# First block of x on ScalarE's transfer queue, and TensorE's warm-up on a tile of zeros with one product less

## The chip, the cores and the metric

The kernel runs on one core of one Trainium2 chip. Five engines work side by side and each runs its own list of instructions in order: TensorE (PE, with its weight loads as PEld), VectorE (DVE), ScalarE (ACT), GpSimd (POOL) and SyncE (SP). Transfers are issued by an engine's queue and are carried by the core's 16 DMA engines. The metric is the device time of one execution in microseconds (us), lower is better.

## The reference

One block of tokens x (2048 tokens of 448 values) goes through two attentions of 16 heads with 28 values each, and the two results are mixed by a gate per token.

```
g = sigmoid(sum(x * gate_w))
A:  q, k, v = split(x @ A_wqkv)                       # 16 heads of 28
    phi(t) = [softmax(t @ w_phi), softmax(-(t @ w_phi))]
    a = (phi(q) (phi(k)^T v)) / (phi(q) sum(phi(k)) + 1e-6) @ A_wo
B:  q, k, v = split(x @ B_wqkv)
    b = softmax(q k^T / sqrt(28)) v @ B_wo
out = g * a + (1 - g) * b
```

All inputs are float32. A is a linear attention, B an ordinary one with 2048 x 2048 scores per head.

## The kernel before

Values are split into a high part in a short format (`fp32r`) and a low rest, and a product is made of three passes: high times high, high times the weight's low part, and x's low part times high. x lies transposed in SBUF as `XH` (high) and `XL` (low), in four blocks `b` of 128 of the 448 input values (the last block holds 64 of them twice, high and low) and four tiles `t` of 512 tokens.

The stages are: the projection of q and k of attention B (28 units, a unit being 128 outputs by 512 tokens; results go out to DRAM as `qkd`); beside it and behind it the folding of `w_phi` into the A weights (`pwk`), the values and features of attention A, and the row maxima for B's softmax (`mx_unit`, from products `pmd` and `pmb`); then the long loop of B over scores (`g`), exponentials (`p`) and values (`pv`); last the output projection.

The order on TensorE, VectorE, ScalarE and GpSimd is that of the program text (`tc.manual_schedule` names these four). SyncE is not among them: the order of its queue, which issues the loads and stores, is set by the framework's planner from its own estimate of when each one is wanted and when its buffer is free. Each transfer counts on one of eight semaphores in turn, so a transfer also waits until the one eight places before it has landed.

`first_units` (L580 to L616) is the start. It issues eight loads of 256 KB, by turns a block of the weights `wqkB` (L585) and a block of x's first tile (L586), into `first_raw0` to `first_raw3`, and then the two loads of x's second tile (L132, by `x_loads`), which reuse the buffers of the first blocks. While these travel, TensorE runs eight 128 x 128 products of the identity matrix `ident` with itself into a PSUM bank that is overwritten later (L591); `ident` is made by GpSimd. Then, for each block b, ScalarE casts the weights to their high part (L594), VectorE (block 0) or ScalarE (the others) casts x (L595), VectorE forms the two low parts (L596, L598, and L601 for the last block), and TensorE runs 12 products of 128 x 512 (8 for the last block) into four PSUM banks (L608). After the four blocks the results are copied and written out by `keep_qk` (L546, L547, L548), through four buffers `ev` that are free again when their write has landed.

The other units follow in `proj_qk` (L109). Around them the transfers of SyncE's queue bring x's third and fourth tile (L132, L323), `phi_s` (L626), the weights `wkA` to be folded (`wtk`, L355), the second weights `wB1` in two halves (L132, cast at L143), `wvA`, and two small constants `sel_s` and `mask_s` (L633, L634). GpSimd's one small copy at L353 writes into `wtk` from `phi_s`, so the loads of `wtk` wait for it and it waits for `phi_s`. Later `qp`, `kp` and `kt` are loaded from `qkd` (L176), GpSimd subtracts (L206), and the first `pmd` product (L260) uses them.

`red` is a 128 x 128 tile that VectorE sets to zero at the start (L163) and that the row maxima use later.

Of the kernel before, what the change touches and what calls it, by code (L numbers as in the profile page):

```python
# [17 lines left out]
P = 128  # L18
# [18 lines left out]
def f32(ap):  # L37
    return ap.bitcast(F32)
# [3 lines left out]
def gated_mix_kernel(ctx, tc, xT, wqkB, wvB, wvA, wkAT, wqAT, phi, woA, woB,  # L42
# [7 lines left out]
    nc = tc.nc  # L50
# [12 lines left out]
    def ps_s(nm):  # L63
        return ps.tile([P, 512], F32, tag="s", name=nm, bufs=psn[0])

    def ps_pv(nm):
        return ps.tile([P, 512], F32, tag="pv", name=nm, bufs=1)

    def ps_mx(nm):
        return ps.tile([P, 512], F32, tag="mx", name=nm, bufs=psn[1])  # L70
# [12 lines left out]
    ident = const.tile([P, P], F32, name="ident")  # L83
# [78 lines left out]
    red = mxp.tile([P, 128], F32R, name="red", bufs=1)  # L162
# [380 lines left out]
    def keep_qk(m, t, pq, ev):  # L543
        tt = slice(t * 512, (t + 1) * 512)
        e = ev.tile([P, 2, 512], F32R, tag="ev", name=f"ev{t}_{m}")
        nc.scalar.copy(e[:, 0, :], pq)  # L546
        nc.vector.tensor_sub(e[:, 1, :], pq, f32(e[:, 0, :]))  # L547
        nc.sync.dma_start(qk_d[m * P:(m + 1) * P, :, tt], f32(e))  # L548
# [14 lines left out]
    def x_loads(t):  # L563
        loads(("x", t), lambda: load_x(t, 0), lambda: load_x(t, 2))
# [7 lines left out]
    def splits(n):  # L572

        if n % 4 == 1 and n < 12:
            split_x(n // 4 + 1, raws.pop(("x", n // 4 + 1)))
        if n in (13, 15):
            split_part(wB[1], "wB1", 384, (n - 13) // 2)
        take_lows()

    def first_units():  # L580

        raw = [stg.tile([P, 2, 512], F32, tag="stg", name=f"first_raw{b}") for b in range(3)]
        raw.append(f32(ev.tile([P, 2, 512], F32R, tag="ev", name="first_raw3")))
        for b in range(4):
            nc.sync.dma_start(raw[b][:, 0, :], wqkB[:, b, :512])  # L585
            nc.sync.dma_start(raw[b][:, 1, :], xT[:, b, :512])  # L586
        x_loads(1)
        pqs = [ps_s(f"pqk0_{m}") for m in range(3)] + [ps_pv("pqk0_3")]
        later.extend(ps_mx(f"pqk_{i}") for i in range(3))
        for _ in range(8):  # L590
            nc.tensor.matmul(pqs[3][:, :P], ident, ident, start=True, stop=True)  # L591
        for b in range(4):
            w, x = wB[0][:, :, b, :], XH[:, b, :512]
            nc.scalar.copy(w[:, 0, :], raw[b][:, 0, :])  # L594
            (nc.scalar.copy if b else nc.vector.tensor_copy)(x, raw[b][:, 1, :])  # L595
            nc.vector.tensor_sub(w[:, 1, :], raw[b][:, 0, :], f32(w[:, 0, :]))  # L596
            if b < 3:
                nc.vector.tensor_sub(XL[:, b, :512], raw[b][:, 1, :], f32(x))  # L598
                todo = [(0, x), (1, x), (0, XL[:, b, :512])]
            else:  # L600
                nc.vector.tensor_sub(x[64:], raw[b][64:, 1, :], f32(x[64:]))  # L601
                todo = [(0, x), (1, x)]
            if b < 3:
                order = [(i, m) for i in range(3) for m in range(4)]
            else:
                order = [(i, m) for m in range(4) for i in range(2)]
            for i, m in order:
                nc.tensor.matmul(pqs[m], w[:, todo[i][0], m * P:(m + 1) * P], todo[i][1],  # L608
                                 start=b == 0 and i == 0, stop=b == 3 and i == 1,
                                 skip_group_check=True)  # L610
        hold = raws[("x", 1)][0][:1, 0, :4]
        splits(1)
        nc.gpsimd.tensor_copy(phi_s[:1, :, 0], hold)
        for m in range(4):
            keep_qk(m, 0, pqs[m], ev)

    later = []
    first_units()
    pkv = ps_pv("pkv")
    for n in range(4, NP):  # L620
# [588 lines left out]
```

## Time and profile before

| what | us |
|---|---|
| median of 3 runs (984.8 to 987.25) | 984.94 |
| the profiled execution's own time | 984.67 |
| its span, first to last instruction | 982.9 |
| TensorE busy | 976.8 (99%) |
| ScalarE busy | 752.8 (77%) |
| VectorE busy | 727.6 (74%) |
| GpSimd busy | 235.4 (24%) |

In the rows shown below, a merged row gives the start, the length, the engine, the line, the operation, what is written from what, the shapes, how many instructions were merged, and in brackets the idle time before it with what ended that. SPq is SyncE's queue issuing a transfer; the length is that of the issue, not of the transfer. A row with "x4: 187/188/333" gives the number of instructions and their shortest, median and longest duration in ns, then the first and last start. A row that begins with two times and a colon is a stretch: its length, the busy time of PE, PEld, DVE, ACT and POOL with the number of instructions, TensorE's granted clock, the share of the DMA engines' time in use, and GB/s. The end of a TensorE row is modelled, so the distance from one start to the next tells more than its length.

### The profile page before, as it was taken

The page shows a single profiled execution, that of the slowest core. Times are in us where ns is not written, and L with a number is a line of the kernel's source. Part 1 is how long each engine was busy: PE and PEld are TensorE (multiplying, and loading weights), DVE is VectorE, ACT ScalarE, POOL GpSimd, SP SyncE. Part 2 cuts the span into 40 slices and gives each one's busy share as a digit, 9 for nine tenths or more (in the row PEclk, how much of TensorE's full clock was granted, in tenths as well). Part 3 has the DMA queues.
Part 4 walks back from the last instruction along what each step waited for, and adds up shares of the span by engine and source line. Part 5 has one row for each costly group of instructions (what it writes and reads, how often), then busy time and mean ns, then how long its engine had stood idle before and what let it go on. Part 6 is the DMA issues. An engine that isn't in the chain of part 4 may idle for free.

```text
span 982.9 us, 22267 instructions
## 1 busy us (share of the span) xinstructions
PE 976.8 (99%) x8384; PEld 606.0 (62%) x8384; DVE 727.6 (74%) x1335; ACT 752.8 (77%) x1442; POOL 235.4 (24%) x224
## 2 busy tenths in 40 slices
PE   9999999999999999999999999999999999999998
PEld 8877877787777665555555555555555555555555
DVE  5566767799765678888888888888888888885112
ACT  5455655578776688898898898898898898897662
POOL 1235435578734710031011011011011011010010
PEclk9999999999999999999999999999999999999999
DMA  9973110013233233121132121122231222100441
GB/s 306 324 233 117 37 53 32 23 47 99 73 103 111 89 121 126 40 59 40 65 91 69 42 61 41 60 77 71 70 82 41 64 63 63 40 24 31 141 150 57
DMA packets 56139, 84.47 MB, mean 86 GB/s; under 512 B 17216, under 2 KB 23984, under 8 KB 56032
## 3 DMA queue, kind: packets, MB, share of 16 engines
q1 hardware_dynamic: 56032, 83.06, 27.1%
q8 instruction: 66, 1.08, 0.5%
q14 instruction: 41, 0.34, 0.1%
HBM read 54.86 MB, written 27.78 MB: 84 GB/s over the span
## 4 chain that ended last, share of the span: by engine, by line
PE 96%; DVE 3%; issue 0%; ACT 0%; POOL 0%; DVEq 0%; POOLq 0%; ACTq 0%
PE g L830 29%; PE pv L975 27%; PE pqk L109 6%; PE poa L109 4%; PE pk L127 4%; PE pva L127 4%; PE g L288 3%; PE pmd L260 3%; PE pob L109 3%; PE pvb L127 2%; PE pvb L109 2%; PE pq L109 2%; PE pn L507 1%; PE pqk L608 1%; PE pft L495 1%; PE poL L1008 1%
## 5 line engine op out<-in xcount | busy, mean ns | idle before, releaser
L838 ACT ACTIVATE p<-g 128x512 f32<-128x512 f32 x1020 | 525.7, 608 | 82.5 <-PE g L830 81.8
L295 DVE TENSOR_REDUCE part<-g 128x1 f32<-128x512 f32 x704 | 442.2, 683 | 84.4 <-PE g L288 83.8
L830 PEld LDWEIGHTS g<-qst,kst 32*128 32x128 f32 x3060 | 220.9, 182 | 215.3 <-DVE part L295 194.4
L830 PE MATMUL g<-qst,kst 32*128 32x512 f32 x3060 | 337.6, 419 | 0.1
L975 PE MATMUL pv<-p,vb 128*32 128x512 f32 x2048 | 273.0, 604 | 0.0
L288 PE MATMUL g<-kc,qc 28*128 28x512 f32 x704 | 233.2, 494 | 0.0
L394 POOL TENSOR_TENSOR oUb<-oUb,rsb 128x512 f32<-128x512 f32 x15 | 19.3, 1286 | 490.9 <-DMA rsb<-rdb 423.8
L265 DVE CUSTOM_DVE_ANT_0 rl<-pmb,rl 128x512 f32<-128x512 f32 x160 | 103.2, 682 | 43.7 <-ACT rl L264 43.7
L264 ACT ACTIVATE rl<-pmd 128x512 f32<-128x512 f32 x160 | 87.4, 601 | 31.3 <-PE pmb L260 29.0
L288 PEld LDWEIGHTS g<-kc,qc 28*128 28x128 f32 x704 | 86.2, 181 | 0.2
L975 PEld LDWEIGHTS pv<-p,vb 128*32 128x32 f32 x2048 | 40.5, 108 | 66.1 <-issue 64.8
L109 PE MATMUL pqk<-XH,wB 128*128 128x512 f32 x192 | 59.1, 396 | 0.0
L546 ACT CAST ev<-pqk 128x512 fp32r<-128x512 f32 x28 | 16.1, 589 | 39.8 <-PE pqk L109 28.7
L986 DVE SCALAR_TENSOR_TENSOR acc<-pob,gate,acc 128x448 f32<-128x448 f32 x12 | 8.2, 684 | 48.3 <-PE pob L109 48.3
L109 PE MATMUL poa<-woA_s,oTa 128*128 128x448 f32 x192 | 43.5, 375 | 0.0
L260 PE MATMUL pmb<-kp,qp 28*128 28x512 f32 x160 | 42.0, 495 | 0.7 <-DVE part L265 0.3
L547 DVE TENSOR_TENSOR ev<-pqk,ev 128x512 fp32r<-128x512 f32 x28 | 19.0, 689 | 31.0 <-ACT ev L546 31.0
L109 PEld LDWEIGHTS pqk<-XH,wB 128*128 128x128 f32 x192 | 35.4, 188 | 8.6 <-issue 1.5
L260 PE MATMUL pmd<-kp,qp 28*128 28x512 f32 x160 | 39.9, 494 | 0.0
L127 PE MATMUL pk<-wkA_s,XH 128*128 128x448 f32 x128 | 39.4, 381 | 0.0
L109 PEld LDWEIGHTS poa<-woA_s,oTa 128*128 128x128 f32 x192 | 34.9, 188 | 6.3 <-issue 2.9
L127 PE MATMUL pva<-wvA_s,XH 128*128 128x450 f32 x128 | 37.8, 371 | 0.0
(154 smaller groups left out, 1085.8 us busy)
## 6 DMA issues: line engine op xcount, KB each, us to landing
qkd<-ev SPq DMA_DIRECT2D x28, 512.0 KB
qst<-qkd SPq DMA_DIRECT2D x64, 112.0 KB
kst<-qkd SPq DMA_DIRECT2D x64, 112.0 KB
od<-oTb SPq DMA_DIRECT2D x48, 112.0 KB
rsa<-rda SPq DMA_DIRECT2D x8, 512.0 KB
oL<-od SPq DMA_DIRECT2D x8, 512.0 KB
rsb<-rdb SPq DMA_DIRECT2D x15, 256.0 KB
gad<-ga SPq DMA_DIRECT2D x16, 224.0 KB
```

What stands on the lines that cost most here:

```text
L109: nc.tensor.matmul(dst, l, r, start=i == 0, stop=i == len(todo) - 1)
L127: nc.tensor.matmul(dst[:, :n], l, r, start=i == 0, stop=i == len(todo) - 1, skip_group_check=True)
L260: nc.tensor.matmul(pm[j], qc[js, qt * P:(qt + 1) * P], kc[js, :], start=True, stop=True, tile_position=(32 * i, 0))
L264: nc.scalar.activation(rl, pm[i], AF.Relu)
L265: nc.vector.tensor_tensor_reduce(rl, pm[2 + i], rl, 1.0, LOWEST, ALU.add, ALU.max, part[:, col + i:col + i + 1])
L288: nc.tensor.matmul(pm, mxs[("qc", gq)][js, qt * P:(qt + 1) * P], mxs[("kc", gq // NQ, kb)][js, :], start=True, stop=True, tile_position=(3 ...
L295: nc.vector.tensor_reduce(part[:, col:col + 1], pm, AX.X, ALU.max)
L394: (nc.gpsimd if n == 1 else nc.vector).tensor_mul(oU, oU, rs)
L547: nc.vector.tensor_sub(e[:, 1, :], pq, f32(e[:, 0, :]))
L830: nc.tensor.matmul(st[j], kst_of[(gq // NQ, kt // 4)][js, k, (kt % 4) * P:(kt % 4 + 1) * P], qst_of[gq][js, q, :], start=n == 0, stop=n == ...
L838: nc.scalar.activation(p, st[j], AF.Exp, scale=SCALE)
L975: nc.tensor.matmul(pv[32 * j:32 * j + 32, :], vb[kt // 8][:, kt % 8, 4 * g + j, :], pt[j], start=kt == 0, stop=kt == NT - 1, tile_position ...
```

## The change

```
         for b in range(4):
             nc.sync.dma_start(raw[b][:, 0, :], wqkB[:, b, :512])
-            nc.sync.dma_start(raw[b][:, 1, :], xT[:, b, :512])
+            (nc.sync if b else nc.scalar).dma_start(raw[b][:, 1, :], xT[:, b, :512])
         x_loads(1)
         pqs = [ps_s(f"pqk0_{m}") for m in range(3)] + [ps_pv("pqk0_3")]
         later.extend(ps_mx(f"pqk_{i}") for i in range(3))
-        for _ in range(8):
-            nc.tensor.matmul(pqs[3][:, :P], ident, ident, start=True, stop=True)
+        for _ in range(7):
+            nc.tensor.matmul(pqs[3][:, :P], f32(red), f32(red), start=True, stop=True)
```

The load of x's first block is issued by ScalarE as its first instruction, ahead of the table load that its first cast brings. The warm-up products read `red` in place of `ident`, and there are seven. Apart from these, the order on TensorE, VectorE, ScalarE and GpSimd is the same.

On SyncE's queue the planner puts out another order for the first fifty or so transfers. Before (left) and after (right), a name once for each transfer or group:

```
before                                  after
wqkB 0, x 0, wqkB 1, x 1, ... x 3       wqkB 0, wqkB 1, x 1, ... x 3
                                        x tile 3 block 0
x tile 1 (2 loads)                      x tile 1 (2 loads)
x tile 2 first load                     x tile 2 first load
x tile 3 blocks 0, 1                    x tile 3 blocks 1, 2
x tile 2 second load                    x tile 2 second load
x tile 3 blocks 2, 3                    x tile 3 block 3
phi_s, wB1 first half, sel_s, mask_s
qkd x7                                  qkd x8
                                        phi_s, wB1 first half
wtk x1, qkd x1, wtk x3, qkd x2          qkd x1, wtk x4, qkd x1
wB1 second half, qkd, qp, kp, kt        wB1 second half, qkd, qp, kp, kt
qkd x3, wvA x2                          qkd x3, wvA x2, sel_s, mask_s
```

## The prediction

> **What bounds the kernel.** I read the page's busy shares and chain first, then the rows of the first 16 us in order of time, then the waits up to 66 us, because every instruction that the change touches lies before 50 us.
>
> ```profile
> span 982.9 us, 22267 instructions
> PE 976.8 (99%) x8384; PEld 606.0 (62%) x8384; DVE 727.6 (74%) x1335; ACT 752.8 (77%) x1442; POOL 235.4 (24%) x224
> PE 96%; DVE 3%; issue 0%; ACT 0%; POOL 0%; DVEq 0%; POOLq 0%; ACTq 0%
> ```
>
> TensorE carries 96% of the chain, so a moment saved before its first real product reaches the end unless a later wait eats it. The start, as merged rows:
>
> ```profile
> 0.84 0.17 DVE L163 MEMSET red<- 128x128 f32 x1 [0.84 <-PEq L1196]
> 1.02 0.29 POOL masks.py:199 TENSOR_SCALAR_AFFINE_SELECT ident<-ident 128x128 f32<-128x128 f32 x1
> 1.36 3.78 PE L591 MATMUL pqk<-ident 128*128 128x128 f32 x16 [1.36 <-POOL ident masks.py:199]
> 0.74 0.40 SPq L585 DMA_DIRECT2D first_raw<-in_wqkB_dram  x1
> 1.20 0.41 SPq L586 DMA_DIRECT2D first_raw<-in_xT_dram  x1
> 0.74 1.28 ACT L594 ACT_TABLE_LOAD   x1 [0.74 <-PEq L1196]
> 3.39 0.62 ACT L594 CAST wB<-first_raw 128x512 fp32r<-128x512 f32 x1 [1.37 <-DMA first_raw<-in_wqkB_dram]
> 4.03 0.43 DVE L595 CAST XH<-first_raw 128x512 fp32r<-128x512 f32 x1 [3.03 <-DMA first_raw<-in_xT_dram]
> L608 PEldq EVENT_SEMAPHORE  x1: 51/51/51, 4.5 to 4.5; - x1
> ```
>
> The eight warm-up products (two records each) run from 1.36. Their input `ident` ends at 1.02 + 0.29 = 1.31, so an engine starts 0.05 behind what releases it. The weights are there at 3.39 and x at 4.03; the two copies end at 4.01 and 4.46; TensorE passes its one wait at 4.5. So both inputs of the first real product are ready by about 4.5. TensorE in slices of 0.1 to 0.2 us:
>
> ```profile
> 4.51 0.63 PE L591 MATMUL pqk<-ident 128*128 128x128 f32 x2
> 4.73 0.42 PE L591 MATMUL pqk<-ident 128*128 128x128 f32 x1
> 4.80 0.77 PE L608 MATMUL pqk<-XH,wB 128*128 128x512 f32 x1
> 5.37 1.05 PE L608 MATMUL pqk<-XH,wB 128*128 128x512 f32 x2
> 5.80 0.63 PE L608 MATMUL pqk<-XH,wB 128*128 128x512 f32 x1
> 6.23 0.90 PE L608 MATMUL pqk<-XH,wB 128*128 128x512 f32 x3
> 6.50 0.86 PE L608 MATMUL pqk<-XH,wB 128*128 128x512 f32 x3
> 6.73 0.86 PE L608 MATMUL pqk<-XH,wB 128*128 128x512 f32 x3
> ```
>
> A record of the warm-up takes 0.21 (4.51 to 4.73), a product 0.43; the last one holds TensorE to 4.94, and 5.37 - 0.43 = 4.94 is when the first real product really begins (its record at 4.80 is modelled). Real products go at 0.43 up to 6.23, then at 0.27 and 0.23. So TensorE reaches full speed near 6.3, 4.95 after its first work, although the granted-clock column says 1.00 throughout. Before that a microsecond buys 1/0.43 products, later 1/0.23: a microsecond of the slow time is worth 0.23/0.43 = 0.53.
>
> **The change, part by part.**
>
> *Warm-up on `red`.* `red` is set at 0.84 + 0.17 = 1.01 against 1.31 for `ident`: the first product starts at 1.06, 0.30 earlier, with the same shape and thus the same 0.43. One product less is another 0.43. TensorE is free at 4.94 - 0.73 = 4.21. What is late next is the data. `red` is written again only after the score products, which begin at 48.34 (last row below): no wait.
>
> *x's first block on ScalarE's queue.* ScalarE has no work before 3.39 except its table load (1.28). One issue in front of it costs 0.40 and a 0.06 gap, so the load ends near 2.5 and keeps 0.9 of cover; without that cover it would cost up to 0.46. x is issued at 0.74 instead of 1.20, and SyncE's following issues each move 0.46 forward. How two queues share the transfers, no row shows. Ends: the x transfer gains the whole 0.46 (3.57) and the weights lose nothing (3.39), then the copies end at 4.01 and 4.00 and TensorE can start at 4.21, when its warm-up ends; or nothing is gained in bandwidth and the weights, now halved with x, arrive only with it at 4.03, then ScalarE's copy ends at 4.65 and, with the 0.09 between the last copy and the real start allowed by the 4.5 wait, TensorE starts at 4.75. I take 4.45, both landing near 3.7: the rows put both blocks in place within 4.03 of the start from one queue, and the saved issue time brings the pair forward by some 0.3.
>
> [...]
>
> *What the start is worth.* From 4.94 to 4.45 is 0.49 of slow time, times 0.53 = 0.26 us. If full speed still comes at 6.3, that is all; if it comes 4.95 after first work, it comes 0.30 earlier, worth 0.30 x (1 - 0.53) = 0.14 more. I take half of it, 0.07. Sum: -0.33. Ends: 4.21 and the full 0.14 give 0.39 + 0.14 = -0.53; 4.75 and no shift give -0.10.
>
> *Is the work behind it ready?* The next weights set the pace:
>
> ```profile
> 6.06 0.62 ACT L594 CAST wB<-first_raw 128x512 fp32r<-128x512 f32 x1 [2.05 <-DMA first_raw<-in_wqkB_dram]
> 6.76 0.62 ACT L595 CAST XH<-first_raw 128x512 fp32r<-128x512 f32 x1
> 8.35 1.98 PE L608 MATMUL pqk<-XH,wB 128*128 128x512 f32 x8
> 10.75 1.05 ACT L336 CAST XH<-xraw 128x1024 fp32r<-128x1024 f32 x1 [0.68 <-DMA xraw<-in_xT_dram]
> 15.61 0.62 PE L109 MATMUL pqk<-XH,wB 128*128 128x512 f32 x2
> ```
>
> Block 1 is ready at 7.38 and used at 8.35, with me at about 8.0: covered by 0.6. One 256 KB block of the fourth x tile now goes ahead of the second tile's two loads; at the 326 GB/s below that is 0.8 us, so its first copy ends near 10.75 + 1.05 + 0.8 = 12.6 and is used at 15.3: covered.
>
> *SyncE's queue.* The planner's new order also puts the loads of `phi_s` and the first half of `wB1` behind the first eight `qkd` writes, `sel_s` and `mask_s` behind the `wvA` loads, and the first `wtk` load with the other three.
>
> ```profile
> 2.00:16.00 14.00, 14.00 (x61) 12.03 (x61) 9.26 (x14) 8.02 (x14) 0.39 (x2) 1.00 0.95 326
> 16.00:36.00 20.00, 20.00 (x89) 16.54 (x89) 10.86 (x15) 8.83 (x16) 4.20 (x11) 1.00 1.00 343
> 14.53 0.43 SPq L626 DMA_DIRECT2D phi_s<-in_phi_dram  x1
> 15.07 0.39 SPq L132 DMA_DIRECT2D wB_raw<-in_wqkB_dram  x1
> 27.77 0.56 SPq L355 DMA_DIRECT2D wtk<-in_wkAT_dram  x1
> 21.05 0.18 POOL L353 COPY wtk<-phi_s 1x4 f32<-1x4 f32 x1
> qkd<-ev SPq DMA_DIRECT2D x28, 512.0 KB
> 22.98 0.59 ACT L546 CAST ev<-pqk 128x512 fp32r<-128x512 f32 x1 [3.77 <-DMA qkd<-ev]
> 36.24 0.84 ACT L143 CAST wB<-wB_raw 128x768 fp32r<-128x768 f32 x1
> 40.54 1.04 PE L362 MATMUL pwk<-phi_s,wtk 112*128 112x112 f32 x8
> 43.34 3.04 POOL L206 TENSOR_TENSOR kp<-kp,kt 28x512 fp32r<-28x512 f32 x2 [11.56 <-DMA kt<-qkd]
> 48.34 0.50 PE L260 MATMUL pmd<-kp,qp 28*128 28x512 f32 x2
> ```
>
> The transfers are the second bound here: share 1.00 at 343 GB/s (the column before the last and the last). Eight writes of 512 KB are 4.2 MB, 12.2 us. So `phi_s`, read by GpSimd at 21.05, is read near 33.3; GpSimd's copy releases the `wtk` loads, behind which SyncE waits. Four issues at 0.6 to 36; what is then ahead in the transfers, 512 + 384 + 4 x 224 KB = 1.8 MB, is 5.3 us, so `wtk` is there by 33.3 + 5.3 = 38.6, wanted at 40.54 - 0.4. Covered by 1.5; `wB1`, right behind `phi_s`, by about 34.5 against 36.24. Nothing is added to the bytes, and the `qkd` writes come forward by the 580 KB that went behind, 1.7 us, so ScalarE's 3.77 wait at 22.98 shrinks. Behind the `wtk` wait SyncE's next writes and the `kp`, `qp`, `kt` loads move by at most 1 us; GpSimd ends its work on them at 46.38, TensorE wants it at 48.34. `sel_s` and `mask_s` cost 0.9 of issue in front of later loads, inside the same margin. I cost all of it at nothing; without the cover it costs what the `wtk` loads are late, 1 us for 1 us.
>
> **The sum.** -0.33 against the profiled execution's 984.67 (982.9 of span and 1.8 around it): 984.3. The median of the runs shown, 984.94, is 0.27 above that execution, so 984.6 in its terms.
>
> **Rivals.**
>
> *Full speed comes late.* TensorE now pauses from 4.21 to 4.45. If that pause, or zeros as operands, starts the count anew, full speed comes 4.95 after 4.45, at 9.4 and not 6.3: 3.1 x 0.47 = 1.5 lost, less 0.26: 986.2. For it: in the trace full speed came only after work without a gap. Against: the pause is a twentieth of those 4.95. [...]
>
> *x lands late on the other queue (the slower side).* The third transfer of SyncE's queue landed only at 6.06, 2.0 after the second. If x's block falls behind it to 6.06, its copy ends at 6.5, TensorE starts at 6.6 and is slow to 11.5. It would have done (6.3 - 4.94)/0.43 + (11.5 - 6.3)/0.23 = 26 products by then and does 11.5: 14.5 x 0.23 = 3.3 lost, 988.2. It decides from a landing near 5.7 on. For it: only that unexplained 2.0. Against: x is issued first of all on its queue.
>
> *A stall behind SyncE's new order.* If `wtk` comes 5 later than reckoned, TensorE loses 3.5: 988.1; over 0.3% from 4.7 late on. For it: SyncE stands behind a transfer that sits in a full queue. Against: the working above already has full queues.
>
> *The start doesn't move*, if x gains nothing and the weights lose: the end of -0.10, or up to 0.1 slower; no change.
>
> **How the numbers follow.** 0.3% is 2.95 us, about what a measurement of this kernel can tell from no change. My forecast, its bounds and the start that doesn't move have 0.70; full speed late 0.15, also within 0.3%. x late 0.05 and the stall 0.06 end slower by more. Faster by more has no mechanism of this size in the rows; 0.04 for runs that scatter (984.8 to 987.25 are shown). So 0.04, 0.85, 0.11. The range goes from 984.94 - 0.53 with 0.8 below it for a moment of full speed that differs between runs (1.7 us earlier x 0.47) to the late case with 0.3 above: 983.6 to 986.5.
>
> **What would show it.** The warm-up at 1.06, 14 records, free at 4.2; the copies of x and weights both ending near 4.3; the first real products 0.43 apart from about 4.45 on; then 0.23 from near 6.3 (from 9.4 if late); no gap over 0.1 us at the first `pwk` product. The last real product of the first tile would end 0.3 before its 15.6. I am wrong if x's copy waits beyond 4.6, if the weights' copy begins after 4.0, or if TensorE waits between 15 and 50 us.

## The result and the profile after

The changed kernel takes 986.56 us (median of 17 executions, 984.15 to 988.98) against 984.49 us (median of 17, 983.51 to 987.25) for the kernel before: a ratio of 1.002, 95% interval 1.0012 to 1.0029. It is 2.1 us slower. That is inside the 0.3% class that the prediction put at 0.85, but 2 us above the time it forecast and just outside its range, and on the other side of no change.

Of the 17 times four lie at 984.15 to 984.55, none from there to 986.06, eight at 986.06 to 987.85, and five at 988.14 to 988.98. I read them as three groups; the last five are those whose mean granted clock is 0.998, against 0.999 or 1.000 in all others. The profiled execution, 987.85, is of the middle group. Its page (span and the instructions, the busy shares, and the chain by engine):

```profile
span 986.1 us, 22261 instructions
PE 979.3 (99%) x8382; PEld 607.6 (62%) x8382; DVE 727.6 (74%) x1335; ACT 752.4 (76%) x1442; POOL 234.0 (24%) x224
PE 94%; DVE 3%; DMA 1%; issue 0%; ACT 0%; DVEq 0%; ACTq 0%
```

TensorE is the bound as before. Where the 3.2 us of this pair of profiles (982.9 to 986.1) arise is told by four places in the program that every execution passes: the end of the first tile (the first row of L109, 15.61 before), the first `pwk` product (40.54 before), GpSimd's 16 instructions of L433 and ScalarE's 1020 exponentials of L838. For a line, the view gives shortest, median and longest duration in ns, then the first and the last start in us. Before:

```profile
L433 POOL TENSOR_TENSOR featk<-featk,fsumk x16: 1701/1706/1707, 76.1 to 185.4; 128x896 f32<-128x896 f32 x16
L838 ACT ACTIVATE p<-g x1020: 590/603/869, 360.3 to 967.9; 128x512 f32<-128x512 f32 x170
```

and after:

```profile
L433 POOL TENSOR_TENSOR featk<-featk,fsumk x16: 1700/1703/1707, 77.9 to 187.2; 128x896 f32<-128x896 f32 x16
L838 ACT ACTIVATE p<-g x1020: 591/605/887, 363.4 to 971.0; 128x512 f32<-128x512 f32 x170
```

The other two as merged rows of after:

```profile
17.69 0.62 PE L109 MATMUL pqk<-XH,wB 128*128 128x512 f32 x2
42.63 1.04 PE L362 MATMUL pwk<-phi_s,wtk 112*128 112x112 f32 x8
```

The shifts are +2.1 at 15.6, +2.1 at 40.5, +1.8 at 76 and at 185, +3.1 at 360 and +3.1 at 968. So the first 2.1 are complete at the end of the first tile. A further 1.3 comes between 185 and 360, where a load `dena` lands late and VectorE waits for it. It is a piece of the chain (start, length, what):

```profile
291.71 9.47 DMA dena<-oUa
```

Another profile of the same kernel, below, loses nothing there, so the first 2.1 are the matter.

The start of the changed kernel, in merged rows; the last five are TensorE in slices of 0.1 to 0.4 us, so they overlap:

```profile
0.73 0.40 ACTq L586 DMA_DIRECT2D first_raw<-in_xT_dram  x1
1.05 3.35 PE L591 MATMUL pqk<-red 128*128 128x128 f32 x14 [1.05 <-DVE red L163]
1.16 1.28 ACT L594 ACT_TABLE_LOAD   x1 [1.16 <-PEq L1196]
4.64 1.28 ACT L594 CAST wB<-first_raw 128x512 fp32r<-128x512 f32 x2 [2.19 <-DMA first_raw<-in_wqkB_dram]
4.84 0.43 DVE L595 CAST XH<-first_raw 128x512 fp32r<-128x512 f32 x1 [3.84 <-DMA first_raw<-in_xT_dram]
5.41 3.75 PE L608 MATMUL pqk<-XH,wB 128*128 128x512 f32 x8 [1.00 <-DVE XH L595]
5.97 0.63 PE L608 MATMUL pqk<-XH,wB 128*128 128x512 f32 x1
9.39 0.97 PE L608 MATMUL pqk<-XL,wB 128*128 128x512 f32 x2
9.81 0.78 PE L608 MATMUL pqk<-XL,wB 128*128 128x512 f32 x2
10.20 0.40 PE L608 MATMUL pqk<-XL,wB 128*128 128x512 f32 x1
10.43 0.40 PE L608 MATMUL pqk<-XH,wB 128*128 128x512 f32 x1
```

The warm-up is as forecast: 14 records from 1.05, free near 4.2. The data is not. The copy of the weights begins at 4.64 (before: 3.39) and that of x at 4.84 (before: 4.03). The first real product begins at 5.97 - 0.43 = 5.54, 0.6 later than before, after a pause of 1.3 (from 4.20, when the warm-up is over by the distances; by the modelled ends it is 1.00). The records then stand 0.42 and 0.39 apart (9.39, 9.81, 10.20) and 0.23 from 10.20 on: full speed comes near 10.1 and not at 6.3.

By the prediction's two prices (0.53 for a microsecond of later start, 0.47 for a microsecond of later full speed) this is 0.60 x 0.53 + (10.13 - 6.31) x 0.47 = 0.32 + 1.80 = 2.1, which is the shift at 15.6.

### The profile page after: what moved, and what is told of

The parts are those of the page before. It is cut to its first block, busy times and chain, and to the rows that moved or that the text cites. A ratio compares the mean times of both kernels' runs of the same rounds, so it can differ in the third digit from the quotient of the medians.

```text
span 986.1 us, 22261 instructions
## 1 busy us (share of the span) xinstructions
PE 979.3 (99%) x8382; PEld 607.6 (62%) x8382; DVE 727.6 (74%) x1335; ACT 752.4 (76%) x1442; POOL 234.0 (24%) x224
## 4 chain that ended last, share of the span: by engine, by line
PE 94%; DVE 3%; DMA 1%; issue 0%; ACT 0%; DVEq 0%; ACTq 0%
PE g L830 29%; PE pv L975 26%; PE pqk L109 6%; PE pk L127 4%; PE pva L127 4%; PE poa L109 4%; PE g L288 4%; PE pmd L260 3%; PE pob L109 3%; PE pvb L127 2%; PE pq L109 2%; PE pvb L109 1%; PE pqk L608 1%; PE pn L507 1%; PE pft L495 1%; DMA dena<-oUa 1%
## 5 line engine op out<-in xcount | busy, mean ns | idle before, releaser
L838 ACT ACTIVATE p<-g 128x512 f32<-128x512 f32 x1020 | 525.6, 609 | 82.8 <-PE g L830 81.4
L109 PE MATMUL pqk<-XH,wB 128*128 128x512 f32 x192 | 59.1, 396 | 0.0
L109 PE MATMUL poa<-woA_s,oTa 128*128 128x448 f32 x192 | 43.5, 375 | 0.0
L109 PEld LDWEIGHTS pqk<-XH,wB 128*128 128x128 f32 x192 | 35.4, 188 | 8.5 <-issue 1.5
L109 PEld LDWEIGHTS poa<-woA_s,oTa 128*128 128x128 f32 x192 | 34.9, 188 | 6.3 <-issue 2.9
```

Source lines behind the costliest of these rows:

```text
L109: nc.tensor.matmul(dst, l, r, start=i == 0, stop=i == len(todo) - 1)
L838: nc.scalar.activation(p, st[j], AF.Exp, scale=SCALE)
```

## The experiments

The theory from this profile: x and the weights, issued on two queues at once, both land late; TensorE therefore pauses behind its shorter warm-up; and the pause puts full speed off, which costs most of the 2.1. The rivals: the time is lost behind SyncE's new order; zeros as operands do not bring full speed; the mere start of a second queue holds up the loads; a shorter warm-up costs by itself, pause or not.

**x's load on ScalarE's queue alone**, warm-up as before.

```
-            nc.sync.dma_start(raw[b][:, 1, :], xT[:, b, :512])
+            (nc.sync if b else nc.scalar).dma_start(raw[b][:, 1, :], xT[:, b, :512])
```

> x's first block on ScalarE's queue, the warm-up as before (eight products on ident, 1.36 to 4.94). In the changed kernel's profile both first loads landed late (weights' cast at 4.64, x's cast at 4.84, against 3.39 and 4.03), and full speed came at 10.1 instead of 6.3. Theory 'two queues': the two loads share the transfers and land late here too, the casts start at 4.5 or later, the real products at 5.3 or later, so TensorE pauses 0.4 after its warm-up; some executions miss the moment of full speed: 0.3 to 1.5 us slower than before. Theory 'the pause': landing late was chance and only the shorter warm-up hurts: casts near 3.4 to 4.0, and within 0.3 us of before. Theory 'SyncE's order': most of the loss comes from the moved phi_s and wB1 loads, which stay early here: no loss.

Measured: 985.23 (11 executions, 984.62 to 987.92) against 984.44, ratio 1.0011 (1.0003 to 1.002). Its start, merged:

```profile
4.72 0.62 ACT L594 CAST wB<-first_raw 128x512 fp32r<-128x512 f32 x1 [2.27 <-DMA first_raw<-in_wqkB_dram]
4.53 0.43 DVE L595 CAST XH<-first_raw 128x512 fp32r<-128x512 f32 x1 [3.53 <-DMA first_raw<-in_xT_dram]
5.39 2.14 PE L608 MATMUL pqk<-XH,wB 128*128 128x512 f32 x8 [0.44 <-ACT wB L594]
```

The second queue alone makes both loads late, the weights by 1.3 us and x by 0.5, although x was issued 0.46 earlier. With eight products the pause is 0.44, and in this profile full speed was already there: eight products took from 5.39 to 7.4. So the load's part of the change gains nothing, and by the medians costs about 0.8 us. This profile shows no such loss (its first tile ends 0.07 early), so what the median loses must be in other executions. SyncE's order here is that of the changed kernel up to x's fourth tile and that of before from `phi_s` on.

**Seven warm-up products on `red` alone**, x on SyncE's queue.

```
-        for _ in range(8):
-            nc.tensor.matmul(pqs[3][:, :P], ident, ident, start=True, stop=True)
+        for _ in range(7):
+            nc.tensor.matmul(pqs[3][:, :P], f32(red), f32(red), start=True, stop=True)
```

> x's first block back on SyncE's queue, the warm-up of the changed kernel (seven products on red, 1.06 to 4.21). Theory 'two queues': the loads land as before (casts at 3.4 and 4.0), real products start at about 4.55, the pause is 0.35; if that is harmless, 0.3 us faster than before. [...] Theory 'SyncE's order' (phi_s, wB1 late here as in the changed kernel): 1 to 2 us slower with full speed near 6.3.

Measured: 987.72 (5 executions, 986.19 to 989.16) against 984.44, ratio 1.0032 (1.002 to 1.0044). The start did well: the weights at 3.55, x at 4.16, the first tile over at 15.76, 0.15 behind before. The loss stands elsewhere. The planner's order of SyncE's queue changed again, in another way than in the changed kernel: both halves of `wB1` are issued behind the four `wtk` loads, and ScalarE's first copy of `wB1` waits. Merged rows, and then two stretches:

```profile
42.02 0.83 ACT L143 CAST wB<-wB_raw 128x768 fp32r<-128x768 f32 x1 [5.53 <-DMA wB_raw<-in_wqkB_dram]
44.50 1.22 PE L109 MATMUL pqk<-XH,wB 128*128 128x512 f32 x2 [2.77 <-DVE ev L547]
```

```profile
40.90:44.30 3.40, 0.83 (x8) 0.65 (x6) 1.42 (x2) 2.28 (x5) 0.00 (x0) 1.00 0.98 348
44.30:47.70 3.40, 3.20 (x8) 2.53 (x9) 2.14 (x4) 0.69 (x1) 0.51 (x1) 0.50 0.49 172
```

TensorE stands for 2.77 us (ScalarE behind `wB1` copies no results, and no PSUM bank comes free), and then has half its clock for one stretch of 3.4. Together some 4 us: by 76 this profile is 4.1 behind before, and it stays so to the end. So this run doesn't tell what the short warm-up costs by itself, but it shows that the planner's order can carry the whole loss, and that here a stretch of 3.4 at a clock of 0.50 followed the stall of TensorE. The changed kernel, whose order differs, has neither: its copy of `wB1` starts at 38.32 without a wait and the clock is 1.00 there.

**The change with ten warm-up products**, so that there is no pause.

```
-        for _ in range(7):
+        for _ in range(10):
```

> The changed kernel with ten products on red instead of seven, 1.06 to 5.33, so that TensorE does not pause before data that lands as in its profile. Theory 'the pause': full speed comes between 4.5 and 7.9 again, the loss shrinks from 2.1 us to about 0.5 (the late data alone). Theory 'zeros': zeros don't count, full speed stays at 9 to 12, and the loss stays at 2 us or more. Theory 'SyncE's order': the loss stays at 2 us with full speed near 6.

Measured: 984.98 (11 executions, 984.3 to 987.49) against 984.44, ratio 1.0007 (0.9998 to 1.0015).

```profile
4.68 0.62 ACT L594 CAST wB<-first_raw 128x512 fp32r<-128x512 f32 x1 [2.24 <-DMA first_raw<-in_wqkB_dram]
1.05 4.36 PE L591 MATMUL pqk<-red 128*128 128x128 f32 x20 [1.05 <-DVE red L163]
5.36 2.14 PE L608 MATMUL pqk<-XH,wB 128*128 128x512 f32 x8
```

The loads are as late as in the changed kernel, SyncE's order is the same as there, the operands are zeros, and the real products begin no earlier. Only the pause is gone, and 0.5 us is left, which can't be told from nothing. Full speed comes near 5.0 (the eight products take from 5.36 to 7.3). That speaks against SyncE's order (in the changed kernel) and against the zeros as causes. By the time alone it doesn't settle the matter, since the changed kernel itself, run beside it, has an interval that overlaps with this one (next run).

**The changed kernel again**, on the chip of these three runs.

> The changed kernel once more, on the chip and in the rounds of the other three, and a second profile of it. Theory 'two queues': casts again at 4.5 or later. If the late landing was chance, they start before 4.0. Full speed by the theory 'the pause' between 8.9 and 12.3. 1.5 to 2.5 us slower than before.

Measured: 985.25 (12 executions, 984.11 to 988.7) against 984.44, ratio 1.0016 (1.0005 to 1.0026). Seven of the twelve are at 984.11 to 985.29, three at 987.08 to 987.67 and two at 988.66 and 988.7. The profiled one, 984.61, is of the first group:

```profile
4.64 0.62 ACT L594 CAST wB<-first_raw 128x512 fp32r<-128x512 f32 x1 [2.18 <-DMA first_raw<-in_wqkB_dram]
5.39 2.08 PE L608 MATMUL pqk<-XH,wB 128*128 128x512 f32 x8 [0.98 <-ACT wB L594]
7.32 1.08 PE L608 MATMUL pqk<-XL,wB 128*128 128x512 f32 x4
```

and the 3.41 us up to 4.46 as a stretch:

```profile
1.05:4.46 3.41, 3.36 (x14) 3.06 (x14) 0.00 (x0) 1.28 (x1) 1.15 (x2) 1.00 0.73 223
```

The same program, the same late loads, the same pause of 0.98 by the records; but the eight products stand (7.32 - 5.39) / 8 = 0.24 apart from the first one on. Full speed was there at 4.46, before any real product, and the pause did no harm. So a pause of this length doesn't always cost the 2 us: in the first profile full speed hadn't come by then, and it came at 10.13. How many executions lose it differs between the sets: 4 of 17 are near 984.5 in the first and 7 of 12 at 985.29 or less here, and the medians of the one program differ by 1.3.

**The kernel before with four warm-up products**: one queue, SyncE's order and operands as before, only a pause.

```
-        for _ in range(8):
+        for _ in range(4):
```

> The kernel before with four warm-up products instead of eight and nothing else: queue, operands and the order of every queue stay. The warm-up ends at 3.2, the data are there at 4.55 as before, so TensorE pauses 1.3 us, as long as in the changed kernel's profile (4.2 to 5.4). [...] Theory 'two queues alone': the pause is harmless, and as the first real product comes a little earlier the time is the same or 0.2 faster.

Measured: 986.46 (11 executions, 985.11 to 987.7) against 984.23, ratio 1.0022 (1.0013 to 1.0031).

```profile
1.36 2.08 PE L591 MATMUL pqk<-ident 128*128 128x128 f32 x8 [1.36 <-POOL ident masks.py:199]
4.25 0.43 DVE L595 CAST XH<-first_raw 128x512 fp32r<-128x512 f32 x1 [3.25 <-DMA first_raw<-in_xT_dram]
4.83 3.75 PE L608 MATMUL pqk<-XH,wB 128*128 128x512 f32 x8 [1.39 <-DVE XH L595]
8.38 1.91 PE L608 MATMUL pqk<-XL,wB 128*128 128x512 f32 x4
10.08 2.28 PE L608 MATMUL pqk<-XH,wB 128*128 128x512 f32 x8
```

The real products begin when they begin in the kernel before (4.83 against 4.80), and still the first tile ends at 17.65 and the whole is as slow as the change: the products are 0.44 apart up to 8.4 and 0.43 up to 10.1. A pause behind a short warm-up reproduces the loss by itself, without a second queue.

**A 2 KB load on ScalarE's queue** ahead of the first loads, else as before (the load is extra; nothing reads it).

```
+        tiny = mxp.tile([P, 4], F32, name="tiny", bufs=1)
+        nc.scalar.dma_start(tiny, sel)
```

> The kernel before plus a 2 KB load of sel into a tile that nobody reads, issued on ScalarE's queue in the place of the changed kernel's x load; all else as before. For the cause of the late landing. Theory 'starting a second queue holds both up': the weights' cast starts at 4.0 or later although there is nothing to share. Theory 'the two share the transfers': 2 KB take nothing away, casts at 3.4 (weights) and 4.0 (x) as before. The time is near before's.

Measured: one execution, 984.97, against a median of 984.23.

```profile
3.57 0.62 ACT L596 CAST wB<-first_raw 128x512 fp32r<-128x512 f32 x1 [1.13 <-DMA first_raw<-in_wqkB_dram]
4.26 0.43 DVE L597 CAST XH<-first_raw 128x512 fp32r<-128x512 f32 x1 [3.26 <-DMA first_raw<-in_xT_dram]
```

Both loads land about 0.2 later than before (0.18 the weights, 0.23 x); with x's 256 KB on that queue it was 1.25 and 0.81 in the changed kernel's first profile. So in these profiles most of the delay came with the large load and not with the second queue alone. Two stretches of 1.25 us, first before and then the changed kernel (the last number is GB/s), show where the time goes:

```profile
1.50:2.75 1.25, 1.25 (x6) 1.25 (x7) 0.00 (x0) 0.52 (x1) 0.71 (x1) 1.00 0.68 195
1.50:2.75 1.25, 1.25 (x8) 1.25 (x8) 0.00 (x0) 0.95 (x1) 0.70 (x1) 1.00 0.69 92
```

With the two loads on two queues the transfers begin at half the rate: 92 GB/s in this stretch, 195 with one. That is 0.13 MB less, by estimate some 0.3 us at the 382 GB/s that the changed kernel has from 2.75 to 4.00, and a good part of x's delay. Then the two loads share the transfers evenly in the changed kernel's trace (48 packets on each queue from 3.0 to 3.5), so the weights land with x and not ahead of it. Why the transfers begin more slowly, these runs don't tell. One thing differs besides the second queue, and no run takes it apart: SyncE, relieved of x, issues the second block's weights at 1.20 instead of 1.66.

**The change with four warm-up products**: the pause doubled.

```
-        for _ in range(7):
+        for _ in range(4):
```

> The changed kernel with four warm-up products on red instead of seven: warm-up 1.06 to 2.93, data at 5.3, a pause of 2.4 us, too long for an early full speed. Theory 'the pause': the fast executions of the changed kernel (984.1 to 985.3, full speed at 4.5 in one profile) disappear, full speed always comes between 8.7 and 12.1, every execution lies above 985.5 and the median at 986.5 to 987. Theory 'late data alone' : median within 0.5 us of the changed kernel's on the same chip, with fast ones among them.

Measured: 988.04 (5 executions, 986.92 to 988.75) against 984.23, ratio 1.0034 (1.0021 to 1.0046).

```profile
1.06 2.08 PE L591 MATMUL pqk<-red 128*128 128x128 f32 x8 [1.06 <-DVE red L163]
5.54 3.78 PE L608 MATMUL pqk<-XH,wB 128*128 128x512 f32 x8 [2.41 <-ACT wB L594]
```

and two stretches:

```profile
60.80:64.20 3.40, 2.33 (x9) 1.32 (x9) 3.40 (x9) 1.78 (x3) 1.85 (x1) 1.00 0.86 321
64.20:67.60 3.40, 3.40 (x12) 2.18 (x11) 0.37 (x2) 0.03 (x1) 0.00 (x0) 0.50 0.41 154
```

None of the five is near 984.5 any more, as it would be if full speed had come before the pause. The profiled execution loses 1.9 in the first tile and 2.1 more at 64.2 to 67.6, where the clock falls to half for one stretch although TensorE is fully busy in it; in the stretch before, it was busy for 2.33 of 3.4, because it waited for VectorE there. The third group of the changed kernel's executions is most likely this, though none of them was profiled: a mean clock of 0.998 is, by estimate, one such stretch, 3.4 x 0.5 / 986 = 0.0017. It isn't the change's alone: of the 23 executions of the kernel before that stand beside the last two runs below, two have 0.998 as well, 987.31 and 987.63.

**The changed kernel once more**, one profile on the chip of these three runs.

> A further profile of the changed kernel, to see a third moment of full speed: 4.3 to 4.9 (fast, near 984.6) or 8.9 to 12.3 (slow, above 986) by the theory 'the pause'; casts at 4.4 to 4.9 by 'two queues'. A mean clock of 0.998 would show in the trace where TensorE's clock falls again.

Measured: one execution, 987.34.

```profile
5.34 3.75 PE L608 MATMUL pqk<-XH,wB 128*128 128x512 f32 x8 [0.93 <-ACT wB L594]
8.89 1.90 PE L608 MATMUL pqk<-XL,wB 128*128 128x512 f32 x4
10.60 1.59 PE L608 MATMUL pqk<-XH,wB 128*128 128x512 f32 x6
```

Full speed near 10.7, the first tile over at 17.91 (+2.3). The shift is 2.6 at 76 and stays 2.6 to 968; the late `dena` of the first profile isn't here. So this one belongs to that execution and not to the change.

**The warm-up begun on `red`, finished on `ident`, x on SyncE's queue**: of eight products, the first alone reads `red`. With this the planner keeps SyncE's order of before.

```
-        for _ in range(8):
-            nc.tensor.matmul(pqs[3][:, :P], ident, ident, start=True, stop=True)
+        for i in range(8):
+            t = f32(red) if i < 1 else ident
+            nc.tensor.matmul(pqs[3][:, :P], t, t, start=True, stop=True)
```

> The kernel before with the first of its eight warm-up products on red, so that the warm-up runs from 1.06 to 4.64 instead of 1.36 to 4.94; x's block stays on SyncE's queue and every queue keeps its order. No pause, since the data are there at 4.55. Theory 'the pause' and 'two queues': the part of the change that helps, alone: first real product 0.3 earlier (0.16) and full speed 0.3 earlier on average (0.14): 0.3 us faster, which lies within the scatter of such runs; no execution above 986. If an earlier warm-up itself hurts, 1 us or more slower.

Measured: 984.25 (12 executions, 983.73 to 987.12) against 984.79, ratio 0.9995 (0.9986 to 1.0004). The real products begin at 4.84 instead of 4.94; the first tile ends 0.13 earlier. Not distinguishable from before.

**The same with seven products**, a short pause.

```
-        for i in range(8):
+        for i in range(7):
```

> As red1_ident7 with one product less, seven in all as in the changed kernel: 1.06 to 4.21, data at 4.55, a pause of 0.35 with nothing else changed. [...]

Measured: 984.59 (11 executions, 983.76 to 986.01) against 984.79, ratio 0.9996 (0.9987 to 1.0004).

```profile
4.62 2.20 PE L609 MATMUL pqk<-XH,wB 128*128 128x512 f32 x8 [0.21 <-DVE XH L596]
6.66 1.07 PE L609 MATMUL pqk<-XL,wB 128*128 128x512 f32 x4
```

A pause of 0.2 by the records (0.6 by the distances, from 4.20 on) did no harm in this profile, and none of the eleven executions is above 986.01. The earlier start that the change was to bring exists on one queue: 0.2 us, the first real product from about 4.8 by the distances. It is too small to be told from nothing in the time. No version here is shown faster than the kernel before.

The prediction's two prices can now be held against ten profiles. For each: when the first real product begins, when full speed comes (both read from the distances of TensorE's records), the shift of the first tile's end by 0.53 x (start - 4.94) + 0.47 x (full speed - 6.31), with the start in place of the second moment where full speed was there already, and the shift measured against 15.61. The trace has records of the granted clock, and the first begins with full speed: it gives the same moments to 0.01, and 4.46, 4.62 and 4.99 where the table says that full speed was there before the start.

| kernel | start | full speed | reckoned | measured |
|---|---|---|---|---|
| after, first profile | 5.54 | 10.13 | +2.12 | +2.09 |
| after_look | 5.47 | 10.66 | +2.32 | +2.31 |
| after_again | 5.47 | before it | -0.11 | -0.12 |
| queue_alone | 5.50 | before it | -0.08 | -0.07 |
| after_10 | 5.47 | before it | -0.11 | -0.11 |
| ident4_alone | 4.96 | 10.64 | +2.05 | +2.04 |
| after_4 | 5.70 | 9.59 | +1.94 | +1.92 |
| red7_alone | 4.87 | 6.75 | +0.17 | +0.15 |
| red1_ident7 | 4.84 | 6.21 | -0.10 | -0.13 |
| red1_ident6 | 4.78 | 4.91 | -0.74 | -0.79 |

The kernel with the 2 KB load is left out, because there TensorE also waits in the first tile: the second block's weights are cast at 6.52 instead of 6.06.

## Why the prediction was wrong

- **"I take 4.45, both landing near 3.7": this step failed.** The copies begin at 4.64 and 4.84 and the first real product at 5.54. Even the pessimistic end of that step, 4.75, was too early: it supposed that two queues move as many bytes in the same time as one, and that x could at worst keep its 4.03. On two queues both were later than on one: in the trace the weights land 1.25 later and x 0.8 later. The prediction said that no row shows how two queues share the transfers, and then took a value that has a gain in it. In the sum the start was to bring 0.26; it cost 0.32.
- **Full speed "still at 6.3", or 0.15 earlier: wrong, as a consequence, and the larger term.** It came at 10.13; in the sum the moment was to bring 0.07, and it cost 1.80. The rival that full speed comes late is what happened. The prediction wrote its mechanism and priced it at 986.2, 0.4 under the median, and gave it 0.15 because "the pause is a twentieth of those 4.95". For a pause of 0.24 the argument may stand, since the 0.6 of the last run, counted the same way, did no harm; but the pause was 1.3, because of the step above. The two steps were taken as independent, and the second hung on the first.
- **What a pause does.** In the rival the pause starts a count of 4.95 anew. That isn't what the runs showed: from 5.54 it would end at 10.5, but in the profile at 984.61 full speed was there at 4.46, after nothing but the warm-up, and stayed through the same pause. What makes full speed come at 4.46 in one execution of the changed kernel and at 10.13 and 10.66 in two others was not shown.
- **The 1.7 us in the range's lower end**, by which full speed was to come earlier in some runs: no run shows this term. The ten profiles of the table had full speed from 1.85 before the 6.31 (4.46) to 4.35 behind it (10.66). No run shows the widths of the ranges that the expectations give for that moment either; the changed kernel again had 4.46 where 8.9 to 12.3 was expected.
- **The warm-up on `red`** (first product at 1.06, free at 4.21), **ScalarE's table load as cover** (it ends at 2.44, the copy begins at 4.64), **the prices 0.53 and 0.47**: right, the last ones to 0.05 in ten profiles.
- **SyncE's new order costed at nothing: right for this order.** `phi_s` was to be read near 33.3 and is read at 33.77; the first `pwk` product follows the products before it with no gap. But the rival of a stall is real with the order of the other run, where `wB1` and not `wtk` was late: 2.77 of wait and a stretch of half clock.
- **x late on the other queue: partly.** x comes 0.8 late, not 2.0, and the weights come late with it, which that rival didn't have.
- **How small a change can be told.** 0.2% was resolved: the interval, 1.0012 to 1.0029, excludes 1. The prediction said that 0.3% is what can be told; with 17 executions a side it was less. That the median fell just outside the range and not just inside is chance, since the same program gave 985.25 in its second set; the late start and the late full speed are not.

## What to carry to other kernels

Let a warm-up of TensorE last until the data is there: one product too many puts the start off by 0.43 here, worth 0.23 by the prices above, while with a pause of 1.3 the first tile ended 2.1 and 2.3 late in two of three profiles of the changed kernel. So lengthen it when the data's arrival is unsure. Before a load is moved to a second queue to save 0.46 of issue, find out what the pair does together at the start of the kernel, where nothing else is in flight; here each lost more than the issue was worth. And when one step of a working has a wide range, redo the rivals at its ends: with a start at 4.78 a pause of 0.6 did no harm (the last run), with one at 5.54 a pause of 1.3 went with 1.80 of the 2.1.

## What the runs showed of the hardware

- **TensorE's busy time ahead of full speed.** In the 3.41 us before the moment of full speed TensorE was busy for 3.41 in the kernel before (2.90 to 6.31), 3.36 in the changed kernel again (1.05 to 4.46), 3.20 in the last run (1.50 to 4.91) and 3.09 with the seven products on `red` alone (3.34 to 6.75). In the changed kernel's first profile full speed came at 10.13, behind a stretch that was busy throughout; the one ahead of it, with the pause, was busy for 2.40:

```profile
3.30:6.70 3.40, 2.40 (x9) 1.94 (x8) 1.84 (x4) 1.85 (x3) 0.00 (x0) 1.00 1.04 371
6.70:10.10 3.40, 3.40 (x9) 2.62 (x9) 2.64 (x5) 2.03 (x4) 0.00 (x0) 1.00 1.03 391
```

  But its stretch from 1.05 to 4.46 was busy for 3.35, as good as the 3.36 of the changed kernel again, and full speed did not come at 4.46 there. So the busy time of such a stretch doesn't tell by itself when full speed comes.
- **How often it came late.** Of the 30 timed executions of the changed kernel 11 are at 985.29 or less, 37%; three of the 30 were profiled: the one at 984.61 had full speed at 4.46, those at 987.34 and 987.85 at 10.66 and 10.13.
- **The clock falls again within the kernel** in two profiles: to 0.50 from 44.30 to 47.70 with the seven products on `red` alone, behind 3.4 us in which TensorE was busy for 0.83, and to 0.50 from 64.20 to 67.60 with four products in the changed kernel, behind 3.4 us in which it was busy for 2.33. In the next 3.4 it is 1.00 again in both. The 2.33 holds one wait of 0.95, up to 62.19, and not a long stand. But busy time alone doesn't settle a fall: two stretches of the changed kernel's profile at 984.61, the one with the pause behind the warm-up and one near the end, were about as little busy or less (2.48 and 1.91), and half clock did not follow.

```profile
4.46:7.87 3.41, 2.48 (x11) 2.07 (x12) 2.93 (x5) 2.18 (x4) 0.00 (x0) 1.00 1.04 379
977.26:980.67 3.41, 1.91 (x10) 1.43 (x8) 1.08 (x2) 0.00 (x0) 0.00 (x0) 1.00 0.51 184
```

  Behind the wait of 0.95 was VectorE's L144, 2.06 in the profile with four products against 1.10 in the first of the changed kernel; in the one GpSimd's two subtractions of L206 (3.36) began 0.17 before it, in the other 0.6 behind it.

```profile
59.29 3.36 POOL L206 TENSOR_TENSOR kp<-kp,kt 28x512 fp32r<-28x512 f32 x2 [10.52 <-DMA kt<-qkd]
59.46 2.06 DVE L144 TENSOR_TENSOR wvA_s<-wvA_raw,wvA_s 128x900 fp32r<-128x900 f32 x1
```

  The two meet without a fall as well: in the kernel before L144 takes 1.73 beside L206, in after_look 1.76. So the meeting is not enough for a fall; whether it is a part of the cause is a reading, since no run forced or forbade it.
- **Full speed came with zeros as operands too**: at 4.46 in the changed kernel's profile at 984.61, after nothing but products of `red` with itself.
- **The granted-clock column says 1.00 for the slow beginning**: for 0 to 6.31 before and for 0 to 10.13 after, where products stand about 0.43 apart, against 0.23 behind it. The later falls show as 0.50. The trace's clock records only begin with full speed (6.31 before, 10.13 after), and the column counts what has no record as 1.00. The first record is 976.21 long in both profiles.
- **Open**: why the transfers start more slowly when two loads go over two queues, what decides when full speed comes, what makes the clock fall after one stretch and not after another, and the late `dena` of one profile.
